# The last six rows of the first chunk's down projection as three float32r products each, and a new order of quarters in the second chunk

## The chip, the cores and the metric

The kernel runs on one core of one Trainium2 chip. The metric is the time of one execution on the device, in microseconds (us); the median of several runs is compared.

## What is computed

An mLSTM cell over 4 batches, 8 heads, 768 steps and a head width of 40, followed by a feed-forward block on its output: up projection (320 to 2048), exact GELU, down projection (2048 to 320).

```python
for t in range(S):                       # the cell, per batch and head
    m_new = np.maximum(f_gate[:, :, t] + m, i_gate[:, :, t])
    f_stab, i_stab = np.exp(f_gate[:, :, t] + m - m_new), np.exp(i_gate[:, :, t] - m_new)
    C = f_stab * C + i_stab * outer(v_t, k_t);  n = f_stab * n + i_stab * k_t
    y[:, :, t] = sigmoid(o_gate) * (C @ q_t) / np.maximum(np.abs(n @ q_t), 1.0)
x = y.transpose(0, 2, 1, 3).reshape(B * S, H * D)      # 3072 x 320
h = x @ w_in                                            # w_in 320 x 2048
g = 0.5 * h * (1.0 + erf(h / sqrt(2)))
out = g @ w_out                                         # w_out 2048 x 320
```

The weights come as 64-bit floats, which the kernel turns into 32-bit floats itself.

## The kernel before

The 768 steps are cut into 6 chunks of 128. For a chunk, the cell is computed in matrix form for each of the 4 batches: scores (q times k), a weight matrix W of exponentials that masks them, values (scores times v), a read of the state carried over from earlier chunks, and an update of that state. Its output y (128 steps x 4 batches = 512 columns) is turned by TensorE, which gives x, three row blocks (128, 128 and 64 rows, the last one twice) of 512 columns. Then come up, GELU and down of that chunk. The cell of a chunk runs between the matmuls of the feed-forward block of the chunk before it.

TensorE multiplies two kinds of data. Float32 operands are used in the cell and in part of the first chunk. The other matmuls use float32r, a rounded form; to keep the precision, a product is made as three float32r products: high part times high part, rest of x times high part of the weight, and x (rounded) times the low part of the weight. For that, x, g and the weights are split: ScalarE writes the high part (one cast), VectorE the rest (one subtract) and the rounded whole (one copy). Before, weights are scaled in the split and the outputs scaled back. Float32r matmuls read their moving operand in two interleaved halves and leave the result in that order; the output copies put it back.

w_in is held in 10 tiles (line 364), numbers 0 to 4 for the first half of the features and 5 to 9 for the second, where 2 and 7 hold the 64 remaining rows; two quarters of 512 features make a half. w_out is held as 16 rows, each the 128 x 320 block of 128 features, in four tiles of four rows (w_out0 to w_out3). Each weight piece is fetched by a DMA into one of four `bits` buffers (`fetch`, line 383) and turned to 32 bits by two ScalarE operations (`conv_one`, L402 and L403) and two VectorE operations (`conv_two`, L414 and L415), which also asks for a later piece.

The order of all work is written out by hand in strings, FRONT for the first stretch (the cell of chunks 0 and 1 and the feed-forward block of chunk 0), SECOND for the second chunk's block, LATER and LAST for the others. `play` (line 966) reads a string word by word and records the instructions of each word; every engine then runs its own instructions in that order and waits where data or a buffer is not ready. The letters that matter here:

- K and J: `conv_one` and `conv_two` of the next weight piece. Pieces 0 to 9 are w_in, 10 to 25 the rows of w_out.
- F: the next of the 16 rows of the first chunk's down (`first_down_steps`, line 850): four float32 matmuls of 128 x 320, one per batch, into four PSUM banks. After the last row ScalarE copies the banks out (L863) and the SP queue sends them.
- i: split of w_in tiles 5 to 9 into `hi_first` and in place (`split_first`, line 748); h: a copy of those high parts to their later place (`move_first`, L756); Z: split of w_in tiles 0 to 4 (`split_weight`, L745 and L746).
- a and b: high part and low part of a row of w_out (`out_hi`, L894, on ScalarE; `out_lo`, L901, on VectorE).
- u and f: parts of the first chunk's x, and quarters 2 and 3 of its up in float32r (the other two quarters are A and U, in float32).
- X and R: turning one batch of the second chunk's x (L695, with the high part by ScalarE, L705) and its rest and rounded whole (L716 and L717, on VectorE).
- B: the load of a 128 x 1024 tile of M for one batch, from which W is made (L208, L211); `<`: its mask on GpSimd (`mask`, L469); `>`: its 8 exponentials on ScalarE (`weights`, L495). In SECOND these are M and W.
- In SECOND: U, one quarter of up (`Chunk.up`, L920 and L926); g, the GELU of one of 16 rows (L933) and its parts (L934 to L936); d, one row of down with its 12 products (`product`, L940); S, scores of two batches (L567, L573); V, values of one batch (L657); C and h, read and update of the state (L620, L631); G, the sigmoid of the output gate (L505).

Exponentials, sigmoids and GELUs need different tables on ScalarE, so a table load stands at each change between them.

In PSUM, the up of a quarter holds four banks until its four GELUs have read them; in the second chunk, the scores of two batches and the values of batches 0 and 1 use the same banks next. The parts of g stand in a ring of 5 rows in the 16-place tile `g`, which in the first chunk holds the whole of g.

Of the kernel before, what the change touches and what calls it, by code (L numbers as in the profile page):

```python
# [19 lines left out]
BASE = 1.0 + 2.0 ** -12  # L20
LOW = 1.0 / 4097.0
# [10 lines left out]
    M3 f2 S2 V1 Y0 T3 J Y1 C2 e W3 K K K J S3 J C3 f3 K X0 B8 J K R0 B9 h5 J h6 h7 K J V2 K Y2 J J Z Z K  # L32
    K V3 X1 J K r F J h8 h9 (0 )0 F a0 a1 F K b0 b1 F a2 a3 F b2 b3 F F F J K X2 G3 F F J K J Y3 F J K R1 a4 a5 b4 b5 a6 b6 K B10 p + + + + F X3 a7 b7 F J J Z Z R2 R3
    a8 F [1 Z a9 a10 <0 <1 >0 >1 a11 a12 a13 a14 a15 b8 b9 b10 b11 b12 b13 b14 b15 B11 F F """
CELL = "MWGVYXRKQDCSht"
LATER = """
# [9 lines left out]
 U3 + M4 M5 Y0 Y1 D2 D3 K4 W4 W5 g12 t0 d8 g13 d9 g14 X0 t1 R0 d10 g15 X1 R1 C2 h2 O0 O1 d11 V2 Y2 t2 B6 J2 d12 V3 Y3 Q4 L5 B7 d13 X2 t3 R2 d14 X3 R3 d15 + O2 O3"""  # L46
# [8 lines left out]
def kernel(  # L55
# [398 lines left out]
    class Cell:  # L454
# [256 lines left out]
        def split_x(self, b):  # L711
            px = by_set(self.px.pop(b))
            if b == 0:
                parts["x_low"] = fars[0].tile([P, NX + 1, TG], F32R, name="x_low", tag="x_low", bufs=1)
            hi = in_place(parts["x"], b)
            nc.vector.tensor_tensor(out=in_place(parts["x_rest"], b), in0=px, in1=hi, op=OP.subtract)  # L716
            nc.vector.tensor_scalar(out=in_place(parts["x_low"], b), in0=px, scalar1=LOW, scalar2=None, op0=OP.mult)  # L717

# [5 lines left out]
    def products_begin():  # L724

        gate_ctx.close()
        pool = ctx.enter_context(tc.tile_pool(name="parts", bufs=1))
        hi_first.append(pool.tile([P, 5, 2, WP // 2], F32R, name="hi_first", tag="w_sums"))
        parts["x_rest"] = pool.tile([P, NX + 1, TG], F32R, name="x_rest")
        fars.extend([pool])  # L730
# [6 lines left out]
    def home(i):  # L737
        first = {1: 0, 4: 3, 6: 5, 9: 8, 7: 2}.get(i, i)
        if first not in hi_two:
            hi_two[first] = shared([P, 2, 2, WP // 2], F32R, "w_in_hi")  # L740
        return hi_two[first][:, int(i != first)]

    def split(i, w, to, lo):
        w_hi[i], w_lo[i] = to, lo
        nc.scalar.activation(out=to, in_=w, func=AF.Copy, scale=PART * 2.0 ** -12)  # L745
        nc.vector.scalar_tensor_tensor(out=lo, in0=to, scalar=-BASE * 2.0 ** 12, in1=w, op0=OP.mult, op1=OP.add)  # L746

# [6 lines left out]

    def move_first(i):
        nc.scalar.copy(out=home(i), in_=w_hi[i])  # L756
        w_hi[i] = home(i)
# [3 lines left out]
    def first_parts(k):  # L761
# [7 lines left out]
        nc.vector.tensor_scalar(out=parts["x_low"][:, k, :], in0=x, scalar1=LOW, scalar2=None, op0=OP.mult)  # L769

    def first_pair(k):
# [16 lines left out]
        for i in range(2):  # L788
            for e in range(2):
                nc.scalar.activation(out=first_g.t[:, HF * e + 2 * k + i, :].rearrange("p (a t) -> p a t", a=2),  # L790
                                     in_=pus[i][e].rearrange("p (t a) -> p a t", a=2), func=AF.Gelu, scale=4097.0)

    class Hidden:

        def __init__(self):
            self.t = gp.tile([P, NF, TG], F32, name="g", tag="g")

    def up_step(g, sets):
# [16 lines left out]
        for pu, (_, (i0, i1, t0, t1)) in zip(banks, sets):  # L815
            for e in range(2):
                nc.scalar.activation(out=g.t[:, i0 + HF * e:i1 + HF * e, t0:t1], in_=pu[e], func=AF.Gelu)
# [31 lines left out]

    def first_down_steps(g):  # L850
        po = []

        def row(n):

            f = feature[n]
            if n == 0:
                po.extend(ps_mm.tile([P, DM], F32, name="po", tag="ab"[b // 2]) for b in range(B))
            for b in range(B):
                nc.tensor.matmul(po[b], g.t[:, f, b * L:(b + 1) * L], w_row(n), start=(n == 0), stop=(n == NF - 1))  # L859
                if n == NF - 1:  # L860
                    if b % 2 == 0:
                        o_sb = outp.tile([P, 2, DM], F32, name="o_sb", tag="o_sb")
                    nc.scalar.copy(out=o_sb[:, b % 2, :], in_=po[b])  # L863
                    send(0, b, o_sb[:, b % 2, :])
# [3 lines left out]
    class Later:  # L868

        def __init__(self):  # L870
            self.w_hi, self.w_lo = {}, {}

        def begin(self):

            self.ring = gp.tile([P, NF, TG], F32R, name="g_parts", tag="g")

        def g_parts(self, n):

            i = 3 * (n % NM)
            return [self.ring[:, i + k, :] for k in range(3)]  # L880
# [4 lines left out]
        def out_hi(self, n):  # L885

            if n == 0:
                both = fars[0].tile([P, 8, DM], F32R, name="w_out_part", tag="w_sums")
                self.w_hi.update((i, both[:, 4 + i, :]) for i in range(4))
                self.w_lo.update((i, both[:, i, :]) for i in range(4))  # L890
            elif n not in self.w_hi:
                three = raw.tile([P, 3, DM], F32R, name="w_out_hi", tag="bits", bufs=NB)
                self.w_hi.update((n + i, three[:, i, :]) for i in range(3))
            nc.scalar.activation(out=self.w_hi[n], in_=w_row(n), func=AF.Copy, scale=PART * 2.0 ** -12)  # L894

        def out_lo(self, n):

            if n not in self.w_lo:
                four = const.tile([P, 4, DM], F32R, name="w_out_lo", tag=f"w_out{n // 4 - 1}")
                self.w_lo.update((n + i, four[:, i, :]) for i in range(4))  # L900
            nc.vector.scalar_tensor_tensor(out=self.w_lo[n], in0=self.w_hi[n], scalar=-BASE * 2.0 ** 12, in1=w_row(n), op0=OP.mult, op1=OP.add)  # L901

    class Chunk:

        def __init__(self, c, later):
            self.c, self.later, self.pus, self.po = c, later, {}, []
            self.side, self.main = [(((ps_mm, "b"), (ps_mm, "a")), ((ps_h, "h"), (ps_tr, "tr")))[(c + i) % 2] for i in (1, 0)]

        def up(self, q):

            at, r = [5 * (q // 2) + 3 * (q % 2) + x for x in range(NX)], 5 * (q // 2) + 2
# [10 lines left out]
            for i in range(2):  # L922
                for n in range(3):
                    for e in range(2):
                        h = halves[e]
                        nc.tensor.matmul(in_pairs(pus[i][e]), w3(r)[n][h, q % 2, i * P:(i + 1) * P], in_turns(x3[n][h, NX, :]),  # L926
                                         start=False, stop=(n == 2), skip_group_check=True)

        def gelu(self, n):
# [3 lines left out]
            nc.scalar.activation(out=whole, in_=self.pus[n // 4][n % 4 // 2][n % 2], func=AF.Gelu, scale=4097.0)  # L933
            nc.scalar.activation(out=hi, in_=whole, func=AF.Copy, scale=PART)  # L934
            nc.vector.tensor_tensor(out=rest, in0=whole, in1=hi, op=OP.subtract)  # L935
            nc.vector.tensor_scalar(out=low, in0=whole, scalar1=LOW, scalar2=None, op0=OP.mult)  # L936

        def product(self, n, t, k):
            x, w = self.later.g_parts(n)[k], self.later.w_parts(n)[k]
# [19 lines left out]
        def finish(self, t):  # L959
            if t % 2 == 0:  # L960
                self.o_sb = outp.tile([P, 2, DM], F32, name="o_sb", tag="o_sb")
            nc.scalar.activation(out=self.o_sb[:, t % 2, :].rearrange("p (a i) -> p a i", a=2),
                                 in_=self.po[t].rearrange("p (i a) -> p a i", a=2), func=AF.Copy, scale=4097.0)
# [21 lines left out]
    def first_blocks():  # L985
# [3 lines left out]
        for r in (32, 96):  # L989
# [12 lines left out]
                 u=first_parts, f=first_pair, i=split_first, h=move_first)  # L1002
# [52 lines left out]
```

## Time and profile before

| | |
|---|---|
| median of 3 runs | 441.36 us (440.73 to 442.05) |
| the profiled execution | 441.83 us |
| its span, first to last instruction | 440.0 us |
| granted TensorE clock, mean | 1.00 |

PE is TensorE's matmuls, PEld its weight loads, DVE VectorE, ACT ScalarE, POOL GpSimd, SPq the DMA queue that the sync engine issues. A row of a time line has the start in the span, the duration (of a run of equal instructions, from the first start to the last end), engine, line, operation, output and inputs, shapes, the count, and in brackets the idle time before it with what ended it. A row of the list of groups has the count, then total busy time, the mean of one in ns, and idle time before. PE's matmuls overlap, so their pace is read from start to start. A float32 matmul is recorded as two instructions, a float32r matmul as one.

### The profile page before, as it was taken

The page shows a single profiled execution, that of the slowest core. Times are in us where ns is not written, and L with a number is a line of the kernel's source. Part 1 is how long each engine was busy: PE and PEld are TensorE (multiplying, and loading weights), DVE is VectorE, ACT ScalarE, POOL GpSimd, SP SyncE. Part 2 cuts the span into 40 slices and gives each one's busy share as a digit, 9 for nine tenths or more (in the row PEclk, how much of TensorE's full clock was granted, in tenths as well). Part 3 has the DMA queues.
Part 4 walks back from the last instruction along what each step waited for, and adds up shares of the span by engine and source line. Part 5 has one row for each costly group of instructions (what it writes and reads, how often), then busy time and mean ns, then how long its engine had stood idle before and what let it go on. Part 6 is the DMA issues. An engine that isn't in the chain of part 4 may idle for free.

```text
span 440.0 us, 12965 instructions
## 1 busy us (share of the span) xinstructions
PE 431.5 (98%) x5320; PEld 374.9 (85%) x5320; DVE 289.4 (66%) x669; ACT 282.2 (64%) x603; POOL 48.7 (11%) x77
## 2 busy tenths in 40 slices
PE   8989999999999999999999999999999999999996
PEld 7778778877788898988898988898988898979986
DVE  8787777778958497837487837587746586533330
ACT  4979999957977977137977138976147915243441
POOL 3000221030020030120040130040010000000000
PEclk9999999999999999999999999999999999999999
DMA  7998996389951383474384564392552300010001
GB/s 156 205 198 229 214 240 150 85 267 226 201 130 50 69 192 66 106 164 84 62 170 74 104 164 76 62 186 34 106 145 29 48 16 1 17 46 0 1 2 60
DMA packets 162267, 48.81 MB, mean 111 GB/s; under 512 B 147776, under 2 KB 155232, under 8 KB 162208
## 3 DMA queue, kind: packets, MB, share of 16 engines
q1 hardware_dynamic: 161888, 47.65, 50.4%
q8 instruction: 42, 0.69, 0.7%
q10 hardware_dynamic: 320, 0.33, 0.2%
q14 instruction: 17, 0.14, 0.1%
HBM read 43.84 MB, written 9.37 MB: 121 GB/s over the span
## 4 chain that ended last, share of the span: by engine, by line
PE 88%; ACT 6%; DMA 2%; SPq 2%; issue 1%; DVE 1%; ACTq 0%; DVEq 0%
PE po L940 31%; PE pu L920 24%; PE po L859 8%; PE pu L926 7%; PE ph L657 3%; PE ps L567 3%; PE pu L780 2%; PE pf L620 2%; DMA bits<-in_moe_w_in_dram 2%; PE px L695 2%; ACT W L495 2%; SPq L173 1%; PE pf L631 1%; PE pt L529 1%; ACT pow L403 1%
## 5 line engine op out<-in xcount | busy, mean ns | idle before, releaser
L935 DVE TENSOR_TENSOR g_parts<-g_whole,g_parts 128x512 fp32r<-128x512 f32 x80 | 56.2, 702 | 68.9 <-ACT g_parts L934 66.3
L933 ACT ACTIVATE g_whole<-pu 128x512 f32<-128x512 f32 x80 | 47.1, 589 | 66.8 <-PE pu L926 54.4
L940 PE MATMUL po<-w_out_hi,g_parts 128*128 128x320 f32 x480 | 80.7, 308 | 0.0
L940 PEld LDWEIGHTS po<-w_out_hi,g_parts 128*128 128x128 f32 x480 | 67.9, 189 | 4.4 <-issue 3.3
L934 ACT ACTIVATE g_parts<-g_whole 128x512 fp32r<-128x512 f32 x80 | 50.5, 631 | 13.2 <-PE po L940 10.4
L920 PE MATMUL pu<-x_hi,w_in_hi 128*128 128x512 f32 x160 | 48.3, 384 | 0.0
L920 PE MATMUL pu<-x_rest,w_in_hi 128*128 128x512 f32 x160 | 47.6, 379 | 0.0
L940 PE MATMUL po<-w_out_lo,g_parts 128*128 128x320 f32 x240 | 44.4, 299 | 0.0
L469 POOL TENSOR_SCALAR_AFFINE_SELECT W<-W 128x1024 f32<-128x1024 f32 (+2 forms) x20 | 21.2, 1060 | 173.4 <-DMA W<-M_d 170.6
L495 ACT ACTIVATE W<-W,aT 128x128 f32<-128x128 f32 x128 | 38.9, 388 | 1.9 <-POOL W L469 1.8
L940 PEld LDWEIGHTS po<-w_out_lo,g_parts 128*128 128x128 f32 x240 | 36.4, 189 | 0.0
L940 PE MATMUL po<-w_out_part,g_parts 128*128 128x320 f32 x240 | 35.0, 303 | 0.0
L859 PE MATMUL po<-w_out,g 128*128 128x320 f32 x128 | 35.0, 432 | 0.0
L940 PEld LDWEIGHTS po<-w_out_part,g_parts 128*128 128x128 f32 x240 | 32.8, 189 | 1.9 <-issue 1.7
L936 DVE TENSOR_SCALAR g_parts<-g_whole 128x512 fp32r<-128x512 f32 x80 | 34.5, 431 | 0.0
L920 PEld LDWEIGHTS pu<-x_rest,w_in_hi 128*128 128x128 f32 x160 | 30.2, 189 | 4.3
L920 PEld LDWEIGHTS pu<-x_hi,w_in_hi 128*128 128x128 f32 x160 | 29.1, 189 | 3.9 <-issue 0.3
L859 PEld LDWEIGHTS po<-w_out,g 128*128 128x128 f32 x128 | 24.1, 190 | 9.7
L920 PE MATMUL pu<-x_low,w_in 128*128 128x512 f32 x80 | 23.8, 379 | 0.0
L920 PE MATMUL pu<-x_low,w_in_lo 128*128 128x512 f32 x80 | 23.8, 379 | 0.0
L402 ACT ACTIVATE sig<-bits 128x320 f32<-128x320 f32 (+1 forms) x26 | 15.2, 586 | 11.0 <-DMA bits<-in_moe_w_out_dram 5.2
L573 DVE TENSOR_TENSOR W<-ps,W 128x256 f32<-128x256 f32 (+1 forms) x48 | 17.7, 414 | 6.2 <-PE ps L567 6.0
(185 smaller groups left out, 737.0 us busy)
## 6 DMA issues: line engine op xcount, KB each, us to landing
W<-M_d SPq DMA_DIRECT2D x16, 512.0 KB, 5.8
bits<-in_moe_w_in_dram SPq DMA_DIRECT2D x20, 256.0 KB, 5.0
bits<-in_moe_w_out_dram SPq DMA_DIRECT2D x16, 320.0 KB, 5.1
blocks<-kq_d SPq DMA_DIRECT2D x32, 128.0 KB, 3.2
ob<-in_o_gate_dram SPq DMA_DIRECT2D x24, 160.0 KB, 4.4
out_dram<-o_sb SPq DMA_DIRECT2D x36, 80.0 KB, 2.0
wide<-M_d SPq DMA_DIRECT2D x4, 512.0 KB, 5.0
kq_d<-in_k_dram SPq DMA_DIRECT2D x6, 320.0 KB, 4.6
```

The costliest lines, as they stand in the source:

```text
L402: nc.scalar.activation(out=s, in_=hi.bitcast(F32), func=AF.Copy, scale=2.0 ** -112)
L469: nc.gpsimd.affine_select(out=x, in_=x, compare_op=OP.is_ge, fill=1.0e30, base=base, pattern=[[0, H], [1, x.shape[2]]], channel_multiplier=-1)
L495: nc.scalar.activation(out=W[n][:, h, :], in_=src, func=AF.Exp, scale=-1.0, bias=aT[:, self.c, r:r + 1])
L573: nc.vector.tensor_tensor(out=w[r, :, t], in0=ps[i][hip][r, :, t], in1=w[r, :, t], op=OP.mult)
L859: nc.tensor.matmul(po[b], g.t[:, f, b * L:(b + 1) * L], w_row(n), start=(n == 0), stop=(n == NF - 1))
L920: nc.tensor.matmul(in_pairs(pus[i][e]), w3(at[k])[n][:, e, i * P:(i + 1) * P], in_turns(x3[n][:, k, :]), start=(n == 0 and k == 0), stop=F ...
L926: nc.tensor.matmul(in_pairs(pus[i][e]), w3(r)[n][h, q % 2, i * P:(i + 1) * P], in_turns(x3[n][h, NX, :]), start=False, stop=(n == 2), skip ...
L933: nc.scalar.activation(out=whole, in_=self.pus[n // 4][n % 4 // 2][n % 2], func=AF.Gelu, scale=4097.0)
L934: nc.scalar.activation(out=hi, in_=whole, func=AF.Copy, scale=PART)
L935: nc.vector.tensor_tensor(out=rest, in0=whole, in1=hi, op=OP.subtract)
L936: nc.vector.tensor_scalar(out=low, in0=whole, scalar1=LOW, scalar2=None, op0=OP.mult)
L940: nc.tensor.matmul(in_pairs(self.po[t]), x[:, t * L:(t + 1) * L], in_turns(w), start=(n == 0 and k == 0), stop=(n == NF - 1 and k == 2), s ...
```

## The change

1. Rows 10 to 15 of the first chunk's down become three float32r products each. A new step z (`split_g`) makes the parts of one such row of g: one ScalarE cast and a VectorE subtract and copy, into tiles that take the places of quarters of g already used. The weights are the parts of w_out rows 10 to 15. Rows 0 to 9 stay float32, with w_out read in two interleaved halves, since all rows of a bank must leave the same order. The last row goes batch by batch.
2. g of the first chunk is four tiles of four rows instead of one of 16; so is the ring of parts later.
3. The second chunk takes the quarters of up in the order 2, 3, 0, 1, and the rows of w_out accordingly from 8 on. The first two use the w_in tiles 5 to 9, which are split before already; the five splits Z of tiles 0 to 4 move from FRONT into SECOND, three behind U1 and two behind g7. The high parts of tiles 5 to 9 keep a place of their own, and the five copies h are dropped.
4. The splits of w_out rows: 10 to 15 stand before the rows that use them, 8 and 9 at the end of FRONT, 0 to 7 in SECOND in instructions of one to three rows. FRONT has the conversions K and J closer together, with none of the splits between them.
5. The loads of M of batches 0 to 3 (B8 to B11) move behind the last weight fetch, and the exponentials of batches 0 and 1 from FRONT to SECOND, behind the first chunk's output copies. Turn X2 moves from behind row 7 to behind row 3, X3 from behind row 11 to behind row 8.
6. The scales in the splits and outputs (LOW, BASE, 4097) are dropped: the high part of a weight is a plain cast, its low part a plain subtract, the rounded whole a plain copy.

```diff
- ... K X0 B8 J K R0 B9 h5 J h6 h7 K J V2 K Y2 J J Z Z K
- K V3 X1 J K r F J h8 h9 (0 )0 F a0 a1 F K b0 b1 F a2 a3 F b2 b3 F F F J K X2 G3 F F J K J Y3 F J K R1 a4 a5 b4 b5 a6 b6 K B10 p + + + + F X3 a7 b7 F J J Z Z R2 R3
- a8 F [1 Z a9 a10 <0 <1 >0 >1 a11 a12 a13 a14 a15 b8 b9 b10 b11 b12 b13 b14 b15 B11 F F """
+ ... K X0 J K R0 J K J V2 K Y2 J J K
+ K V3 X1 J K r F J K (0 )0 F J K F J F X2 G3 F J K F Y3 R1 J K F p + + + + J F J a10,2 b10,2 z10 a12 b12 F X3 z11 F z12 a13,3 b13,3 F z13 F z14 R2 B8 B9 [1 F z15 R3 F <0 <1 a8 b8 B10 B11 F a9 b9 F"""
...
- U0 K1 Q1 L2 D0 D1 C0 h0 M2 M3 g0 g1 g2 g3 + +
- U1 g4 d0 g5 d1 g6 d2 g7 S0 d3 K2 Q2 L3 W2 W3 G0 G1 G2 G3 +
- U2 + g8 d4 g9 V0 V1 K3 Q3 B4 B5 J0 J1 d5 g10 d6 g11 S2 L4 d7
- U3 + M4 M5 Y0 Y1 D2 D3 K4 W4 W5 g12 t0 d8 g13 d9 g14 X0 t1 R0 d10 ...
+ U0 W0 W1 K1 Q1 L2 D0 D1 C0 h0 M2 M3 g0 g1 g2 g3 + +
+ U1 Z Z Z g4 d0 g5 d1 g6 d2 g7 Z Z S0 d3 K2 Q2 L3 W2 W3 G0 G1 G2 G3 +
+ U2 + g8 d4 g9 V0 V1 K3 Q3 B4 B5 J0 J1 d5 g10 d6 g11 a0,3 b0,3 S2 L4 d7
+ U3 + M4 M5 Y0 Y1 D2 D3 K4 W4 W5 a3 b3 g12 t0 d8 g13 a4,2 b4,2 d9 g14 X0 t1 R0 a6,2 b6,2 d10 ...
...
     def split(i, w, to, lo):
-        nc.scalar.activation(out=to, in_=w, func=AF.Copy, scale=PART * 2.0 ** -12)
-        nc.vector.scalar_tensor_tensor(out=lo, in0=to, scalar=-BASE * 2.0 ** 12, in1=w, op0=OP.mult, op1=OP.add)
+        nc.scalar.copy(out=to, in_=w)
+        nc.vector.tensor_tensor(out=lo, in0=w, in1=to, op=OP.subtract)
...
+    def split_g(n):
+        parts_of = []
+        for i in range(3 * len(first_parts_of), 3 * len(first_parts_of) + 3):
+            if i == len(singles):
+                four = gp.tile([P, 4, TG], F32R, name="g_part", tag=f"g{i // 4 % 3}")
+                singles.extend(four[:, j, :] for j in range(4))
+            parts_of.append(singles[i])
+        hi, rest, low = first_parts_of[n] = parts_of
+        whole = first_g.row(n)
+        nc.scalar.activation(out=hi, in_=whole, func=AF.Copy, scale=PART)
+        nc.vector.tensor_tensor(out=rest, in0=whole, in1=hi, op=OP.subtract)
+        nc.vector.tensor_copy(out=low, in_=whole)
...
-            for b in range(B):
-                nc.tensor.matmul(po[b], g.t[:, f, b * L:(b + 1) * L], w_row(n), start=(n == 0), stop=(n == NF - 1))
+            xs, ws = ((g.row(n),), (w_row(n),)) if n not in first_parts_of else (first_parts_of[n], later.w_parts(n))
+            steps = [(k, b) for k in range(len(xs)) for b in range(B)]
+            for k, b in sorted(steps, key=lambda x: x[::-1]) if n == NF - 1 else steps:
+                nc.tensor.matmul(in_pairs(po[b]), xs[k][:, b * L:(b + 1) * L], in_turns(ws[k]), start=(n == 0 and k == 0),
+                                 stop=(n == NF - 1 and k + 1 == len(xs)), skip_group_check=True)
...
+        def out_hi(self, n, k=1):
+            to = self.out_home(HI_AT[n], k)
+            self.w_hi.update((n + i, to[:, i, :]) for i in range(k))
+            nc.scalar.copy(out=to, in_=w_rows[n // 4][:, n % 4:n % 4 + k, :])
+
+        def out_lo(self, n, k=1):
+            to, hi = self.out_home(LO_AT[n], k), self.out_home(HI_AT[n], k)
+            self.w_lo.update((n + i, to[:, i, :]) for i in range(k))
+            nc.vector.tensor_tensor(out=to, in0=w_rows[n // 4][:, n % 4:n % 4 + k, :], in1=hi, op=OP.subtract)
...
+            self.first = 2 if c == 1 else 0
...
         def up(self, q):
-            at, r = [5 * (q // 2) + 3 * (q % 2) + x for x in range(NX)], 5 * (q // 2) + 2
+            p = (q + self.first) % 4
+            at, r = [5 * (p // 2) + 3 * (p % 2) + x for x in range(NX)], 5 * (p // 2) + 2
...
         def product(self, n, t, k):
-            x, w = self.later.g_parts(n)[k], self.later.w_parts(n)[k]
+            x, w = self.later.g_parts(n)[k], self.later.w_parts((n + 4 * self.first) % NF)[k]
```

More of the change, by code (lines that the diff above doesn't have):

```diff
@@ L768, in first_parts @@
         nc.vector.tensor_tensor(out=parts["x_rest"][:, k, :], in0=x, in1=hi, op=OP.subtract)
[L769 removed]
+        nc.vector.tensor_copy(out=parts["x_low"][:, k, :], in_=x)
     def first_pair(k):
@@ L882, in w_parts @@
         def w_parts(self, n):
             return self.w_hi[n], self.w_hi[n], self.w_lo[n]
[L885 to L894, printed above, removed]
```

71 lines of the change are left out of this document (41 added, 30 removed).

## The prediction, made before the changed kernel was run

> **What bounds the kernel now.** I read the page first (span, busy shares, chain), then a table by stage, then the time lines of TensorE, VectorE and ScalarE around the change.
>
> ```profile
> span 440.0 us, 12965 instructions
> ...
> PE 431.5 (98%) x5320; PEld 374.9 (85%) x5320; DVE 289.4 (66%) x669; ACT 282.2 (64%) x603; POOL 48.7 (11%) x77
> ...
> PE 88%; ACT 6%; DMA 2%; SPq 2%; issue 1%; DVE 1%; ACTq 0%; DVEq 0%
> ```
>
> ```profile
> 86.60:121.50 34.90, 34.90 (x137) 24.75 (x135) 28.98 (x64) 26.04 (x62) 4.53 (x5) 1.00 0.88 223
> 121.50:194.00 72.50, 72.50 (x962) 64.16 (x960) 48.92 (x111) 46.68 (x101) 10.62 (x14) 1.00 0.51 109
> ```
>
> The stage columns are the stretch, its length, then busy time of PE, PEld, DVE, ACT and POOL. 86.6 to 121.5 is the first chunk's down; the next row is the second chunk. PE is busy in all of both, at clock 1.00. So the time is TensorE's own work plus whatever makes it wait: what the change takes from PE is gained in full, and every wait it adds is lost in full.
>
> **The six rows on TensorE.** The down of the first chunk is 16 rows of w_out, each with 4 matmuls of 128x320; a float32 matmul leaves two records.
>
> ```profile
> 86.61 17.39 PE L859 MATMUL po<-w_out,g 128*128 128x320 f32 x64
> 103.84 0.38 PE L695 MATMUL px<-ident,ob 128*128 128x128 f32 x2
> ...
> 121.49 0.84 PE L920 MATMUL pu<-x_hi,w_in_hi 128*128 128x512 f32 x2
> ...
> 137.18 5.16 PE L940 MATMUL po<-w_out_part,g_parts 128*128 128x320 f32 x36
> 142.27 1.57 PE L567 MATMUL ps<-qT,kT 64*64 64x128 f32 x64
> ...
> 170.67 1.25 PE L940 MATMUL po<-w_out_hi,g_parts 128*128 128x320 f32 x8
> 171.75 0.71 PE L940 MATMUL po<-w_out_lo,g_parts 128*128 128x320 f32 x4
> 172.30 0.38 PE L695 MATMUL px<-ident,ob 128*128 128x128 f32 x2
> ```
>
> From start to start (a printed duration overlaps the next matmul), 64 records take 103.84 - 86.61 = 17.23 us: 32 matmuls at 0.538 us. The float32r product of the same shape is in the later chunks: 12 take 172.30 - 170.67 = 1.63 us, 0.136 each; 36 in a row take 5.09, 0.141 with an entry gap. Three products are 0.407 to 0.424 us. Removed: 24 matmuls, 12.92 us. Added: 72 products, 9.78 us (to 10.18). Gain 3.14 us, at least 2.74; I take 3.14, because these rows follow matmuls of the same 128 rows of the array.
>
> The Trainium skill (TensorE: Matmul & The Clock Gate, section Back-to-back issue gap) gives a sustained pace of about 81 ns at 128 columns and 131 ns at 512 in streams with weight loads. Halfway, an estimate of 106 ns for 320 columns, it would make the gain 24 x (0.538 - 0.318) = 5.3 us; the rows above measure 136 ns in just such a stream, so the trace disagrees.
>
> The ten rows that stay float32 now read w_out in two interleaved halves. No float32 matmul before does that. Bounds: nothing, since the products at L940 read so and run at 0.136; or half pace, 40 x 0.538 = 21.5 us. I take nothing: the float32 matmul takes four times as long over the same 320 columns, so it asks less of the read.
>
> **Whether the parts come in time.** Each of the six rows needs g split (one ScalarE cast, a VectorE subtract and copy), and w_out rows 10 to 15 split. In VectorE's order all of this stands behind the conversion of the last w_out row. That ends at 116.05 + 0.49 now:
>
> ```profile
> 91.44 1.37 DVE L677 SCALAR_TENSOR_TENSOR ob<-ob,den 128x320 f32<-128x320 f32 x1
> 93.17 0.49 DVE L414 SCALAR_TENSOR_TENSOR pow<-sig,pow 128x320 uint32<-128x320 uint32 x1 [0.37 <-ACT pow L403]
> ...
> 96.63 0.49 DVE L414 SCALAR_TENSOR_TENSOR pow<-sig,pow 128x320 uint32<-128x320 uint32 x1 [2.44 <-ACT pow L403]
> ...
> 97.99 1.28 DVE L746 SCALAR_TENSOR_TENSOR w_in_lo<-w_in_hi,w_in 128x512 fp32r<-128x512 f32 x2
> ...
> 103.36 0.90 DVE L901 SCALAR_TENSOR_TENSOR w_out_part<-w_out_part,w_out 128x320 fp32r<-128x320 f32 x2 [0.48 <-ACT w_out_part L894]
> 104.95 0.90 DVE L901 SCALAR_TENSOR_TENSOR w_out_part<-w_out_part,w_out 128x320 fp32r<-128x320 f32 x2 [0.69 <-ACT w_out_part L894]
> ...
> 112.39 1.29 DVE L901 SCALAR_TENSOR_TENSOR w_out_lo<-w_out_hi,w_out 128x320 fp32r<-128x320 f32 x3
> 114.19 0.49 DVE L901 SCALAR_TENSOR_TENSOR w_out_lo<-w_out_hi,w_out 128x320 fp32r<-128x320 f32 x1 [0.52 <-ACT w_out_hi L894]
> ...
> 116.05 0.49 DVE L415 SCALAR_TENSOR_TENSOR w_out<-sig,pow 128x320 uint32<-128x320 uint32 x1
> ...
> 118.60 0.55 DVE L716 TENSOR_TENSOR x_rest<-px,x_hi 128x384 fp32r<-128x384 f32 x1
> 119.06 0.55 DVE L717 TENSOR_SCALAR x_low<-px 128x384 fp32r<-128x384 f32 x1
> ```
>
> ```profile
> 92.16 0.50 ACT L402 ACTIVATE sig<-bits 128x320 f32<-128x320 f32 x1 [2.73 <-DMA bits<-in_moe_w_out_dram]
> ```
>
> ```profile
> 85.12 1.80 SPq L211 DMA_DIRECT2D W<-M_d  x1
> ```
>
> ```profile
> L935 DVE TENSOR_TENSOR g_parts<-g_whole,g_parts 128x512 fp32r<-128x512 f32 x80 | 56.2, 702 | 68.9 <-ACT g_parts L934 66.3
> ...
> L936 DVE TENSOR_SCALAR g_parts<-g_whole 128x512 fp32r<-128x512 f32 x80 | 34.5, 431 | 0.0
> ```
>
> The change takes from VectorE ahead of that point: two w_in splits (1.28) and eight w_out splits (0.90 + 0.90 + 1.29 + 0.49 = 3.58) with their ScalarE waits (0.48 + 0.69 + 0.52 = 1.69): 6.55 us. The two waits of 0.37 and 2.44 are for w_out data, late behind the two 512 KB loads of W that the SP queue issues first; these loads move behind the last w_out fetch, another 2.81. So the last conversion should end at 116.5 - 9.4 = 107.1. Behind it stand, from start to start: three split instructions for six rows (0.90 + 0.49 + 1.29 = 2.7 at most), five subtract-and-copy pairs before the last one and that one (6 x 0.95 = 5.7, by 702 and 431 ns less the overlap of neighbours), and one x split (0.95): 9.35 us, so the last row's parts are there at 116.5. PE comes to that row at 121.5 - 3.1 - 1.63 = 116.7 and needs the third part some 0.3 later. It fits, with 0.5 us to spare; earlier rows have as much or more, and the last x split is done at 117.4, when the second chunk's up starts at 118.4. Cost taken: nothing. If the conversion ends later than 107.6, each us costs one. Dropping the five moves of w_in parts and moving the W exps only frees ScalarE. The tiles of g that the parts are written to come free in time: the last one needs PE's row 12, whose second product ends near 113.0, and VectorE asks for it at 115.5.
>
> One thing may eat this slack: a W mask on GpSimd, next to which a 0.49 us operation took 1.37 (the first row above, beside the row below). The mask starts 6.25 us after its load is issued (85.12 to 91.37); the loads move behind the last x load, to about 108, and so the masks to about 114, beside the last parts: 0 to 1 us, in the rival on lateness.
>
> ```profile
> 91.37 1.09 POOL L469 TENSOR_SCALAR_AFFINE_SELECT W<-W 128x1024 f32<-128x1024 f32 x1 [23.95 <-DMA W<-M_d]
> ```
>
> **What the second chunk pays.** Quarters 2 and 3 first means that the five w_in splits of quarters 0 and 1 are done inside it: three casts ahead of gelu 4 on ScalarE, two behind gelu 7.
>
> ```profile
> 87.76 1.67 ACT L756 CAST w_in_hi<-hi_first 128x512 fp32r<-128x512 f32 x3
> ...
> 101.71 1.12 ACT L756 CAST w_in_hi<-hi_first 128x512 fp32r<-128x512 f32 x2
> ...
> 133.98 0.60 ACT L933 ACTIVATE g_whole<-pu 128x512 f32<-128x512 f32 x1 [3.62 <-DVE g_parts L936]
> ...
> 136.64 0.60 ACT L933 ACTIVATE g_whole<-pu 128x512 f32<-128x512 f32 x1 [0.24 <-PE pu L926]
> ...
> 141.35 0.63 ACT L934 ACTIVATE g_parts<-g_whole 128x512 fp32r<-128x512 f32 x1 [0.51 <-PE po L940]
> 142.00 1.28 ACT L495 ACT_TABLE_LOAD   x1
> ...
> 152.24 0.60 ACT L933 ACTIVATE g_whole<-pu 128x512 f32<-128x512 f32 x1
> 152.87 0.63 ACT L934 ACTIVATE g_parts<-g_whole 128x512 fp32r<-128x512 f32 x1
> 153.41 0.58 ACT L933 ACTIVATE g_whole<-pu 128x512 f32<-128x512 f32 x1
> ```
>
> ```profile
> 154.09 1.33 PEld L657 LDWEIGHTS ph<-vb,W 128*32 128x32 f32 x128 [0.17 <-ACT g_whole L933]
> ```
>
> The casts cost 1.67 + 1.12 = 2.79 us. ScalarE has 0.24 + 0.51 us of waits in that stretch, and small ones of some 0.2 in all, so the table load at 142.00 slips by 1.8. The scores step, which starts at 142.27, takes the bank of gelu 7: that ended at 141.35 - 0.51 = 140.84, and 1.67 - 0.24 - 0.2 = 1.2 later is 142.1, just in time. From there to gelu 8 at 152.24 ScalarE runs without a wait (exps, sigmoids, two more table loads). The values step at L657, 64 matmuls for each of two batches, takes the PSUM banks of gelu 8 and 9: gelu 8 ends at 152.84, 1.25 before the first batch starts; gelu 9 at 153.99, and the second batch starts half of 1.33 us into the step, at 154.76, 0.77 later. A slip of 1.8 passes both: 0.55 us on the first, 1.0 on the second in all. I add 1.0 for a PE wait there, with 0 (casts hidden) and 1.8 (whole slip) as its ends. What is late next, the gelus 10 and 11, waits for PE already, so it moves with PE; nothing more is lost.
>
> The W exps of batches 0 and 1 (16, with two table loads) now run behind the first chunk's output copies, which makes gelus 0 and 1 some 1.8 later; the 3.62 us that ScalarE waits at 133.98 cover it. The splits of w_out rows 0 to 9 that move into the last two quarters stand before gelus whose data PE brings later still. Scales that fall away, and copies in place of scaled copies of the same shape, I put at nothing.
>
> **Sum.** -3.14 + 1.0 = -2.1 us. The profiled execution's span goes from 440.0 to 437.9; it took 441.83 in all, 0.47 over the median of 441.36. Against the median: 439.3 us.
>
> **Rivals.**
> 1. The casts are hidden, PE doesn't wait at the values step: 441.36 - 3.14 = 438.2. For it: ScalarE's other small gaps in 136 to 142. Against: the 0.77 us of slack is short against 2.79 us of casts. 0.14.
> 2. The parts come 0.5 to 3 us late (masks on GpSimd, data of the last w_out rows, which now wait on 8 rotating DMA slots): 439.8 to 442.3, middle 441.0. For it: only 0.5 us to spare. Against: two of the added splits are wide instructions and cheaper than the sum has them. 0.20.
> 3. Slower: the last w_out conversion does not move forward, since the fetches and not VectorE pace it, and stays near 116.5. Then everything behind it ends at 125.9, the second chunk's up starts at 127.2 instead of 121.5, and with 1.0 the time is 441.36 + 5.7 + 1.0 = 448.1. It decides from 109.7 (no gain left); 0.3% slower from 111.0. For it: ScalarE's waits for data of 2.73 us (92.16). Against: they sit right behind the W loads, which go. 0.12.
> 4. The products don't pay: paced by their weight loads they would take 3 x 0.189 = 0.567 us, more than 0.538.
>
> ```profile
> L940 PEld LDWEIGHTS po<-w_out_hi,g_parts 128*128 128x128 f32 x480 | 67.9, 189 | 4.4 <-issue 3.3
> ```
>
> Then 24 x 0.029 = 0.7 is lost: 441.36 + 0.7 + 1.0 = 443.1. Against it: twelve loads in 1.63 us, so loads overlap. With the interleaved float32 reads (up to 441.36 - 2.1 + 21.5 = 460.8): 0.04.
>
> **How the numbers follow.** The sum 0.50 (its own range 438.7 to 439.9), rivals 0.14, 0.20, 0.12 and 0.04. The predicted time is the sum's. The range 438.0 to 441.6 takes in the sum, rival 1 and most of rival 2, about 0.8. 0.3% is 1.3 us, about what a measurement tells from no change: faster means under 440.0. Faster: 0.50 less 0.02, 0.14, and 0.05 of rival 2: 0.67. Same: 0.02 and most of rival 2 with a little of rival 3: 0.18. Slower: 0.15.
>
> **What would show it.** Right: 72 products in about 9.8 us behind ten rows at 0.538 x 4; the second chunk's first up 3.1 us earlier, at 118.4; ScalarE's table load before the second pair of W exps slipping by 1.8 against PE; a PE wait of about 1 us in all at the values step, put down to g_whole; then a constant distance to the end. Wrong: PE waits for g_part or w_out_part in the first chunk's down (rival 2 or 3, by where the last w_out conversion ends: 107 or 116), no wait at the values step (rival 1), or float32 rows slower than 2.15 us each (rival 4).

## The result, and the profile after

| | before | after |
|---|---|---|
| median, compared on one chip | 441.0 us (5 runs) | 446.89 us (5 runs) |
| ratio after to before | | 1.0124, interval 1.0105 to 1.0143 |
| the profiled execution, its span | 441.83, 440.0 us | 446.04, 444.3 us |

The change makes the kernel 1.24% slower (4.6 to 6.3 us); the forecast was 439.3 us. The page of after, its span and its busy times:

```profile
span 444.3 us, 13025 instructions
...
PE 435.9 (98%) x5344; PEld 376.6 (85%) x5344; DVE 296.6 (67%) x674; ACT 283.1 (64%) x597; POOL 50.3 (11%) x77
```

PE is busy 4.4 us longer than before (431.5), though the six rows should have taken 3.1 us from it. Where that is, TensorE's time line of the first chunk's down shows, matmuls first and then weight loads (start, duration, engine, line, operation, shapes, count, idle time before):

```profile
86.04 11.04 PE L878 MATMUL po<-w_out,g 128*128 128x320 f32 x32
96.91 0.38 PE L697 MATMUL px<-ident,ob 128*128 128x128 f32 x2
...
97.24 13.76 PE L878 MATMUL po<-w_out,g 128*128 128x320 f32 x40
110.83 0.38 PE L697 MATMUL px<-ident,ob 128*128 128x128 f32 x2
```

```profile
85.93 0.64 PEld L878 LDWEIGHTS po<-w_out,g 128*128 128x128 f32 x3
...
113.53 0.19 PEld L878 LDWEIGHTS po<-w_out_part,g_part 128*128 128x128 f32 x1
113.87 8.34 PEld L878 LDWEIGHTS po<-w_out_part,g_part 128*128 128x128 f32 x61
122.46 1.38 PEld L878 LDWEIGHTS po<-w_out_part,g_part 128*128 128x128 f32 x10 [0.24 <-DVE g_part L866]
123.79 0.33 PEld L952 LDWEIGHTS pu<-x_hi,hi_first 128*128 128x128 f32 x2
```

32 records of the float32 rows take 96.91 - 86.04 = 10.87 us, 40 take 13.59: 0.340 a record, 0.680 a matmul, where it was 0.538. Ten rows are 40 matmuls, so 40 x 0.142 = 5.7 us are lost. The 72 products take 123.79 - 113.53 = 10.26 us with one wait of 0.24, so 0.139 each: the gain of the six rows is there, 12.92 - 10.02 = 2.9 us. The down as a whole, from its first weight load to that of the second chunk's first up, grows from 34.95 to 37.86 us (before: the first two of the three rows below; after: 85.93 to 123.79).

```profile
86.51 3.53 PEld L859 LDWEIGHTS po<-w_out,g 128*128 128x128 f32 x14
...
121.46 0.46 PEld L920 LDWEIGHTS pu<-x_hi,w_in_hi 128*128 128x128 f32 x2
...
162.03 0.33 PEld L920 LDWEIGHTS pu<-x_hi,w_in_hi 128*128 128x128 f32 x2
```

A second loss lies in the second chunk: from its first up (U0) to its fourth (U3) it took 162.03 - 121.46 = 40.57 us and takes 42.55. After's weight loads, with the waits, then VectorE and GpSimd there:

```profile
147.97 0.30 PEld L952 LDWEIGHTS pu<-x_hi,w_in_hi 128*128 128x128 f32 x2 [0.36 <-PE po L972]
...
156.78 0.69 PEld L659 LDWEIGHTS ph<-vb,W 128*32 128x32 f32 x64 [0.28 <-ACT g_whole L965]
157.93 0.69 PEld L659 LDWEIGHTS ph<-vb,W 128*32 128x32 f32 x64 [0.46 <-ACT g_whole L965]
...
166.34 0.30 PEld L952 LDWEIGHTS pu<-x_hi,w_in_hi 128*128 128x128 f32 x2 [1.05 <-PE po L972]
```

```profile
145.81 1.29 DVE L748 TENSOR_TENSOR w_in_lo<-w_in,w_in_hi 128x512 fp32r<-128x512 f32 x2
147.11 3.08 DVE L575 TENSOR_TENSOR W<-ps,W 128x256 f32<-128x256 f32 x8
...
162.58 1.57 DVE L967 TENSOR_TENSOR g_parts<-g_whole,g_parts 128x512 fp32r<-128x512 f32 x1
...
164.42 1.14 DVE L931 TENSOR_TENSOR w_out_part<-w_out,w_out_part 128x960 fp32r<-128x960 f32 x1
165.49 1.40 DVE L575 TENSOR_TENSOR W<-ps,W 128x256 f32<-128x256 f32 x4
```

```profile
162.48 1.14 POOL L471 TENSOR_SCALAR_AFFINE_SELECT W<-W 128x1024 f32<-128x1024 f32 x1 [27.26 <-DVE g_parts L967]
```

The wait at the values (156.78 and 157.93) was forecast. Those at U2 (147.97) and U3 (166.34) were not: quarters U2 and U3 use the PSUM banks of the scores, which come free when VectorE has multiplied them into W (L575; PE's own row of U3 names that line), and now a w_in split (1.29 us) and a w_out split (1.14 us) stand ahead of these multiplies. At 162.58 a subtract, 0.69 us elsewhere, also takes 1.57 beside a GpSimd mask.

A third thing went wrong without costing much yet. ScalarE and VectorE in the conversion of the last w_out rows, and the SP queue:

```profile
98.35 0.49 ACT L404 ACTIVATE sig<-bits 128x320 f32<-128x320 f32 x1 [2.45 <-DMA bits<-in_moe_w_out_dram]
...
101.52 0.49 ACT L404 ACTIVATE sig<-bits 128x320 f32<-128x320 f32 x1 [2.21 <-DMA bits<-in_moe_w_out_dram]
...
107.91 0.50 ACT L404 ACTIVATE sig<-bits 128x320 f32<-128x320 f32 x1 [2.99 <-DVE w_out L417]
```

```profile
109.45 0.49 DVE L417 SCALAR_TENSOR_TENSOR w_out<-sig,pow 128x320 uint32<-128x320 uint32 x1
```

```profile
90.13 1.74 SPq L173 DMA_DIRECT2D wide<-in_k_dram  x2
91.92 1.31 SPq L173 DMA_DIRECT2D vb<-in_v_dram  x2
93.34 1.07 SPq L175 DMA_DIRECT2D ob<-in_o_gate_dram  x1
94.50 0.56 SPq L394 DMA_DIRECT2D bits<-in_moe_w_out_dram  x1
...
98.73 4.13 SPq L175 DMA_DIRECT2D ob<-in_o_gate_dram  x1
102.96 0.57 SPq L394 DMA_DIRECT2D bits<-in_moe_w_out_dram  x1
```

The last conversion ends at 109.94, not at 107.1: ScalarE still waits 2.45 and 2.21 us for w_out. In front of the fetch at 94.50 and those behind it stand loads of k, v and the gate for a later chunk (from 90.13). Another gate load, at 98.73, stands in front of the last fetch, but both waits were over before that fetch was issued at 102.96, and the last conversion, at 107.91, waited for VectorE; that this load cost anything is not shown. PE came to row 10 only at 113.5, so the delay stayed hidden behind the slow float32 rows.

Two stages, then: +2.91 in the down and +1.98 in the second chunk, 4.9 us; the stretch before the down was 0.58 shorter in this execution (85.93 against 86.51), which gives the span's 4.3; from U3 to the end both take 278.0 us.

### The profile page after: what moved, and what is told of

The parts are those of the page before. It is cut to its first block, busy times and chain, and to the rows that moved or that the text cites. A ratio compares the mean times of both kernels' runs of the same rounds, so it can differ in the third digit from the quotient of the medians.

```text
span 444.3 us, 13025 instructions
## 1 busy us (share of the span) xinstructions
PE 435.9 (98%) x5344; PEld 376.6 (85%) x5344; DVE 296.6 (67%) x674; ACT 283.1 (64%) x597; POOL 50.3 (11%) x77
## 4 chain that ended last, share of the span: by engine, by line
PE 85%; ACT 8%; DVE 3%; issue 2%; DMA 1%; SPq 1%; DVEq 0%; ACTq 0%
PE po L972 29%; PE pu L952 22%; PE po L878 8%; PE pu L958 6%; PE ph L659 3%; PE pu L778 2%; PE ps L569 2%; ACT W L497 2%; PE pf L622 2%; PE px L697 2%; PE pu L809 2%; PE pf L633 1%; PE cold L250 1%; DMA ob<-in_o_gate_dram 1%; PE ps L553 1%
## 5 line engine op out<-in xcount | busy, mean ns | idle before, releaser
L972 PE MATMUL po<-w_out_part,g_parts 128*128 128x320 f32 x960 | 143.8, 304 | 0.0
L972 PEld LDWEIGHTS po<-w_out_part,g_parts 128*128 128x128 f32 x960 | 131.8, 189 | 6.4 <-issue 4.6
L968 DVE CAST g_parts<-g_whole 128x512 fp32r<-128x512 f32 x80 | 34.7, 434 | 0.0
L952 PE MATMUL pu<-x_hi,w_in_hi 128*128 128x512 f32 x80 | 24.4, 386 | 1.0 <-DVE W L575 0.8
L878 PEld LDWEIGHTS po<-w_out,g 128*128 128x128 f32 x80 | 15.0, 190 | 11.1
L952 PE MATMUL pu<-x_hi,hi_first 128*128 128x512 f32 x80 | 23.9, 380 | 0.0
L952 PE MATMUL pu<-x_rest,hi_first 128*128 128x512 f32 x80 | 23.8, 379 | 0.0
L952 PE MATMUL pu<-x_rest,w_in_hi 128*128 128x512 f32 x80 | 23.8, 379 | 0.0
L575 DVE TENSOR_TENSOR W<-ps,W 128x256 f32<-128x256 f32 (+1 forms) x48 | 17.7, 413 | 4.5 <-PE ps L569 4.3
L707 ACT ACTIVATE x_hi<-px 128x384 fp32r<-128x384 f32 x20 | 9.8, 491 | 16.3 <-PE px L697 15.8
L416 DVE SCALAR_TENSOR_TENSOR pow<-sig,pow 128x320 uint32<-128x320 uint32 (+1 forms) x26 | 15.5, 595 | 5.1 <-ACT pow L405 5.1
```

Source lines behind the costliest of these rows:

```text
L416: nc.vector.scalar_tensor_tensor(out=p, in0=s, scalar=3, in1=p, op0=OP.logical_shift_left, op1=OP.bitwise_or)
L575: nc.vector.tensor_tensor(out=w[r, :, t], in0=ps[i][hip][r, :, t], in1=w[r, :, t], op=OP.mult)
L878: nc.tensor.matmul(in_pairs(po[b]), xs[k][:, b * L:(b + 1) * L], in_turns(ws[k]), start=(n == 0 and k == 0), stop=(n == NF - 1 and k + 1 = ...
L952: nc.tensor.matmul(in_pairs(pus[i][e]), w3(at[k])[n][:, e, i * P:(i + 1) * P], in_turns(x3[n][:, k, :]), start=(n == 0 and k == 0), stop=F ...
L968: nc.vector.tensor_copy(out=low, in_=whole)
L972: nc.tensor.matmul(in_pairs(self.po[t]), x[:, t * L:(t + 1) * L], in_turns(w), start=(n == 0 and k == 0), stop=(n == NF - 1 and k == 2), s ...
```

## The experiments

The table holds, for each, the ratio of its time to that of before on the same chip with its interval, the down (first weight load of row 0 to that of U0) and the stretch from U0 to U3, both from the profiled execution. The times differ from what the two stages add up to by up to 1.1 us: even in before and versions 1 and 2, whose program is the same up to there, the down begins between 86.5 and 88.9 us. So costs of 1 us and less are read from the stages.

| version | ratio | down, us | U0 to U3, us |
|---|---|---|---|
| before | 1 | 34.95 | 40.57 |
| after | 1.0124 (1.0105 to 1.0143) | 37.86 | 42.55 |
| 1 before, rows read interleaved | 1.0212 (1.0175 to 1.0250) | 43.92 | 40.64 |
| 2 before, rows read evens, then odds | 1.0039 (1.0021 to 1.0058) | 36.34 | 40.71 |
| 3 after, float32 rows read in order | 1.0055 (1.0029 to 1.0080) | 34.52 | 42.55 |
| 4 after, whole down in order | 1.0048 (1.0028 to 1.0068) | 35.21 | 42.55 |
| 5 after, splits behind the scores | 1.0065 (1.0043 to 1.0088) | 37.59 | 41.43 |
| 6 as 3 and 5, later loads | 0.9941 (0.9923 to 0.9960) | 31.95 | 42.37 |
| 7 as 3 and 5, w_in splits early | 0.9990 (0.9968 to 1.0012) | 34.87 | 40.55 |
| 8 all repairs (3, 5, 6, 7) | 0.9922 (0.9900 to 0.9945) | 31.95 | 40.44 |
| 9 as 8, whole down in order | 0.9939 (0.9912 to 0.9966) | 32.73 | 40.49 |
| 10 as 8, float32 rows interleaved | 1.0077 (1.0049 to 1.0105) | 37.59 | 40.47 |
| 11 before, later loads | 0.9998 (0.9984 to 1.0013) | 34.96 | 40.68 |

**1. Is it the read?** The kernel before, with nothing but the read (and the columns put back in the output copy):

```diff
- nc.tensor.matmul(po[b], g.t[...], w_row(n), start=(n == 0), stop=(n == NF - 1))
+ nc.tensor.matmul(in_pairs(po[b]), g.t[...], in_turns(w_row(n)), start=(n == 0), stop=(n == NF - 1), ...)
```

> The kernel before with one thing of the change alone: all 16 float32 rows of the first chunk's down read w_out in two interleaved halves (and the output copies put the columns back). Theory (the interleaved read is what slows the float32 matmul, from 0.538 to 0.68 us): 64 matmuls take 0.142 us more each, the stretch from the first of them to the second chunk's first up grows by 9.1 us, and the time goes from 441.0 to about 450. Rival (the read costs nothing, and the slow rows in the changed kernel come from what runs beside them there, DMA or VectorE): the rows stay at 0.538 us and the time stays within 0.5 us of 441.0.

```profile
89.02 21.91 PE L859 MATMUL po<-w_out,g 128*128 128x320 f32 x64
110.77 0.38 PE L695 MATMUL px<-ident,ob 128*128 128x128 f32 x2
```

The interleaved read takes columns 0, 160, 1, 161 and so on. 64 records take 21.75 us: 0.680 a matmul, as in after, with everything around it as in before. The down grows by 8.97 us, the time by 9.4 (451.71 against 442.31). The rival, that something beside them slows the rows, falls.

**2. What in the read?** The same with another order of the columns, 0, 2, 4 and so on, then 1, 3, 5:

```diff
+ nc.tensor.matmul(po[b].rearrange("p (a t) -> p a t", a=2), ..., w_row(n).rearrange("p (t a) -> p a t", a=2), ...)
```

> The kernel before, its 16 float32 rows reading w_out as all even columns and then all odd ones (steps of 8 bytes, never alternating between two places 640 bytes apart). Theory A (any step other than to the next word slows the float32 read): a matmul takes about 0.68 us as with the interleaved halves, and the time is about 9 us above that of before. Theory B (only the alternation between two distant places costs): 0.538 us and no change. A value between would say that the two effects add.

```profile
87.59 18.09 PE L859 MATMUL po<-w_out,g 128*128 128x320 f32 x64
105.52 0.38 PE L695 MATMUL px<-ident,ob 128*128 128x128 f32 x2
```

17.93 us for 32 matmuls, 0.560 each. Steps of 8 bytes cost 0.022 us, alternating between places 640 bytes apart 0.142: neither theory holds alone, but most of the loss comes with the alternation. Other distances than 640 bytes were not tried, so whether the distance matters is open.

The Trainium skill (Advanced Engine Details and Errata, section Memory Cachelines) says that SBUF is read in lines of 16 bytes and that a read keeps its pace if the next access falls into the same line. By that rule the halves hit a new line at every element and the evens every second time, and the float32 times of these two runs agree with it (0.142 and 0.022 lost). The float32r products of runs 8 and 9 below do not: 0.138 in halves, 0.149 in order.

**3. Can the rows be mended alone?** In after, the ten float32 rows read in order and write PSUM in the interleaved order:

```diff
+ if len(xs) == 1:
+     nc.tensor.matmul(po[b].rearrange("p (t a) -> p a t", a=2), xs[k][...], ws[k].rearrange("p (a t) -> p a t", a=2), ...)
+     continue
```

> The changed kernel, its ten float32 rows reading w_out in order again and writing PSUM in the interleaved order instead, so that the 72 products can add to them unchanged. Theory: the cost sits on the side of the read, the 40 matmuls go back to 0.538 us and 5.7 us are given back; since PE then comes to the six rows at about 107.8 and not 113.5, it waits 0 to 2.5 us for their parts (the last w_out conversion ended at 109.9): 441.2 to 443.7. Rival (any order of the columns that is not the same on both sides slows the float32 matmul): no gain, 446.9.

```profile
86.94 8.78 PE L879 MATMUL po<-w_out,g 128*128 128x320 f32 x32
95.56 0.38 PE L697 MATMUL px<-ident,ob 128*128 128x128 f32 x2
...
107.44 0.41 PE L697 MATMUL px<-ident,ob 128*128 128x128 f32 x2 [0.62 <-DVE x_low L719]
...
110.47 0.81 PE L882 MATMUL po<-w_out_part,g_part 128*128 128x320 f32 x4 [0.36 <-ACT g_part L864]
111.72 8.15 PE L882 MATMUL po<-w_out_part,g_part 128*128 128x320 f32 x58 [0.44 <-DVE g_part L865]
120.03 1.63 PE L882 MATMUL po<-w_out_part,g_part 128*128 128x320 f32 x10 [0.17 <-DVE g_part L866]
```

8.62 us for 16 matmuls, 0.539 each: for this matmul the read side is what costs; writing PSUM in steps costs nothing. Of the 5.7 us the down gives back only 3.3 (37.86 to 34.52): PE now comes to row 10 at about 109.9 and waits for the parts. The late conversions are laid bare. The time is 2.2 us over before (444.50 against 442.31 here).

**4. And the float32r products?** In after, all of the first down in order (`po[b]`, `ws[k]` as they are).

> The changed kernel with the whole first down, the float32 rows and the 72 float32r products, reading w_out in order and writing PSUM in order. Theory (only the float32 rows are slow when interleaved, the products take 0.136 us either way): the same as the run with the float32 rows alone put in order, 441.2 to 443.7. Rival (the products need the interleaved read for their pace): they take longer than 0.136 us each, and every 0.01 us more costs 0.72 us.

The same time as run 3, but 68 products took 9.94 us, 0.146 each, against 0.139: the rival has a part of it. Run 9 repeats this where no wait is mixed in.

**5. What delays U2 and U3?** In after, the last two w_in splits and the VectorE half of the first w_out split moved behind the scores (S0, S2) in SECOND:

```diff
- ... d2 g7 Z Z S0 d3 ...      ... g11 a0,3 b0,3 S2 L4 d7
+ ... d2 g7 S0 Z Z d3 ...      ... g11 a0,3 S2 L4 b0,3 d7
```

> The changed kernel with two steps of the second chunk behind the scores step and not ahead of it: the last two w_in splits, and the VectorE half of the first w_out split. Theory (the waits of 0.4 us at quarter U2 and 1.1 us at U3 come from VectorE, which does these splits ahead of the multiplies of the scores that free the PSUM banks): both waits go, up to 1.3 us are gained, 445.6 to 446.0. Rival (the banks are late for another reason, ScalarE's gelus or the GpSimd masks): the waits stay and so does the time, 446.9.

```profile
157.62 0.81 PE L659 MATMUL ph<-vb,W 128*32 128x41 f32 x64 [0.42 <-ACT g_whole L965]
158.76 0.81 PE L659 MATMUL ph<-vb,W 128*32 128x41 f32 x64 [0.34 <-ACT g_whole L965]
```

Both waits at U2 and U3 are gone, U0 to U3 falls by 1.12 us to 41.43. (The time is 3.1 us over before, 445.40 against 442.31, where after has 5.9; the two stages account for 1.4 of that gain.) What stays, 0.86 over before, is the wait at the values (above).

At U3 the split does not act alone. The multiplies start 3.36 us after the scores in after, with a wait of 1.05 on the weight loads; 3.18 after them in run 6 below, with 0.88; 1.66 in run 5, with none. From these, an estimate: the first 2.3 us are free. The w_out split is 1.07 of after's 3.36 us and the stretch of the subtract 0.88, so either alone would have cost 0.2 at most. In run 5 the split is moved, and the mask falls later too (164.15, beside no subtract).

**6. Why are the parts late?** Runs 3 and 5 together, and the loads that turns X1 and X2 issue put behind the fetch of the last w_out row:

```diff
- if self.c == 1 and b < NQ: load(n + NLD, 1, 3)
- if self.c == 1: load(n + NLD, 3, 4)
+ if self.c == 1:
+     put_off.extend([lambda: load(n + NLD, 1, 3)] * (b < NQ) + [lambda: load(n + NLD, 3, 4)])
+     if b in (0, NQ): run_off()
...
- ... X2 G3 F J K F Y3 R1 J ...
+ ... X2 G3 F J ] K F Y3 R1 J ...          # ]: run_off
```

> The changed kernel with the float32 rows reading in order (as in the run before), the second chunk's two steps moved behind the scores step (as there), and the loads of the chunk after next that the output turns X1 and X2 issue moved on the SP queue behind the fetch of the last w_out row. Theory (the parts of rows 10 to 15 come late because those loads hold up the w_out fetches, so that ScalarE and VectorE wait some 3 us for data): the last w_out conversion ends at 107 to 108 and not at 110.2, PE's waits of some 2.7 us in front of and within the products fall to under 0.5, and against the kernel before the time is 1 to 2 us shorter, about 440.5 where before takes 442. Rival (VectorE's own queue sets the end of the conversions, not the data): the conversions end at 109.5 or later, the waits stay, and the time is 0.5 to 1.5 us longer than that of before.

```profile
105.54 0.49 DVE L417 SCALAR_TENSOR_TENSOR w_out<-sig,pow 128x320 uint32<-128x320 uint32 x1
```

```profile
107.69 10.18 PE L888 MATMUL po<-w_out_part,g_part 128*128 128x320 f32 x72
...
159.97 0.67 PE L962 MATMUL pu<-x_hi,w_in_hi 128*128 128x512 f32 x2 [0.66 <-DVE W L581]
```

The last conversion ends at 106.03, the 72 products run without a wait, and the down falls to 31.95, 3.00 under before. The time is 2.3 us under before (439.28 against 441.57), a little more than expected. A wait of 0.66 is back at U3, though no split stands there. By the trace, the masks on GpSimd now fall beside VectorE's two copies ahead of the multiplies, which take 1.31 us each instead of 0.42 (no run moves the masks alone; in run 8 the mask starts at 157.21, behind both copies, and the wait is gone):

```profile
156.03 1.31 DVE L978 CAST g_parts<-g_whole 128x512 fp32r<-128x512 f32 x1
...
157.87 1.31 DVE L978 CAST g_parts<-g_whole 128x512 fp32r<-128x512 f32 x1
```

```profile
155.47 1.59 POOL L477 TENSOR_SCALAR_AFFINE_SELECT W<-W 128x1024 f32<-128x1024 f32 x1 [26.48 <-PE po L982]
157.79 1.90 POOL L477 TENSOR_SCALAR_AFFINE_SELECT W<-W 64x1024 f32<-64x1024 f32 x2 [0.72 <-DMA W<-M_d]
```

**7. What does the values step wait for?** Runs 3 and 5 together, with the five w_in splits at the end of FRONT, where ScalarE waits for PE, and none in SECOND:

```diff
- ... B10 B11 F a9 b9 F
+ ... B10 B11 F a9 b9 Z Z Z Z Z F
...
- U1 Z Z Z g4 d0 g5 d1 g6 d2 g7 S0 Z Z d3 ...
+ U1 g4 d0 g5 d1 g6 d2 g7 S0 d3 ...
```

> The changed kernel with the float32 rows reading in order, the VectorE half of the first w_out split behind the scores step, and all five w_in splits of quarters 0 and 1 done at the end of the first chunk's down, where ScalarE waits 4 to 5 us for PE, and not within the second chunk. Theory (the five casts, 2.8 us of ScalarE, make gelus 8 and 9 late and cost PE 0.7 to 1 us at the values step): the two PE waits put down to g_whole go, the stretch from the second chunk's first up to its U3 goes back from 41.4 to 40.6 us as in the kernel before, and the time is within 0.5 us of before's (442). Rival (the casts only fill gaps; the gelus are late because of PE or VectorE): the stretch stays at 41.4 and the time is 1 us above before's.

```profile
153.69 1.56 PE L659 MATMUL ph<-vb,W 128*32 128x41 f32 x128
```

One run of 128 matmuls without a wait, and U0 to U3 is 40.55, as before. So the five splits cost 0.88 us there (run 5 against 7). Their subtracts on VectorE move as well; that it is the casts is read from the two waits, put down to ScalarE's g_whole.

**8. All repairs together.**

> All three: float32 rows reading in order, the five w_in splits at the end of the first chunk's down with the first w_out split behind the scores step, and the later loads behind the last w_out fetch. If the three costs (interleaved reading 5.7 us, late parts 2.7, waits in the second chunk 2.0) are separate and complete, what is left is the gain of the six rows, 24 x 0.538 - 72 x 0.136 = 3.1 us: 2 to 3.1 us under before, about 439.5 where before takes 442. If one of them only moves the wait elsewhere, the time stays within 1 us of before's.

```profile
108.85 9.97 PEld L888 LDWEIGHTS po<-w_out_part,g_part 128*128 128x128 f32 x72
118.76 0.33 PEld L962 LDWEIGHTS pu<-x_hi,hi_first 128*128 128x128 f32 x2
```

438.63 us against 441.57, 0.78% faster than before, the lowest ratio here, though its interval overlaps those of versions 6 and 9. The down is 3.00 us shorter, the second chunk as long as before to 0.13 us: the three costs were all there was in these two stages.

**9 and 10. Each read order, with nothing else in the way.** Version 8 with the whole down in order:

> The version with all three repairs, but the whole first down reading and writing in order, its 72 float32r products too. Theory (a float32r product loses without the interleaved read what the float32 matmul wins: in the run with everything in order 68 products took 9.94 us, 0.146 each, against 0.139 interleaved): no wait hides it now, the 72 products take about 10.5 us and not 9.95, and the time is 0.5 us above that of the version with all three. Rival (the 0.146 came from waits within that run): the products take 9.95 us and the time is the same.

```profile
108.47 10.73 PEld L884 LDWEIGHTS po<-w_out_part,g_part 128*128 128x128 f32 x72
119.17 0.33 PEld L957 LDWEIGHTS pu<-x_hi,hi_first 128*128 128x128 f32 x2
```

72 products in 10.70 us against 9.91 in version 8: 0.149 against 0.138. The down is 0.78 longer; in the time the difference lies within the intervals. Version 8 with the float32 rows interleaved as in the change:

> The version with all three repairs, but its ten float32 rows reading in two interleaved halves again, as in the change. Theory (the cost of the read adds to whatever else holds): the first down grows from 31.95 to 37.6 us, 40 x 0.142 = 5.7 more, and the time is about 2.8 us above that of before, 0.6% slower. Rival (with the waits gone, part of it is hidden): less than 1 us above before.

```profile
88.27 0.64 PEld L884 LDWEIGHTS po<-w_out,g 128*128 128x128 f32 x3
...
125.86 0.32 PEld L958 LDWEIGHTS pu<-x_hi,hi_first 128*128 128x128 f32 x2
```

The down is 37.59, 5.64 more than in version 8, and the time 2.7 us over before (444.86 against 442.19). The interleaved read alone makes the change a loss.

**11. Do the later loads pay by themselves?** The kernel before, with the loads of run 6 put off in the same way.

> The kernel before with the loads of the output turns X1 and X2 moved on the SP queue behind the fetch of the last w_out row, and nothing else. Theory (the order of the loads matters only because the six rows need their parts by 107 us; in the kernel before PE never waits there): no change, within 0.3% of before. Rival (the later loads are a gain by themselves, and the best version owes its time to them and not to the six rows): 1 us or more under before.

No change (442.17 against 442.47). The later loads are no gain here by themselves.

## Why the prediction was wrong

- **The float32 rows: wrong, and the step that failed.** "I take nothing: the float32 matmul takes four times as long over the same 320 columns, so it asks less of the read." It was 5.7 us (run 10: 5.64; run 1: 0.680 against 0.538 a matmul). The products at L940, which read that way at full pace, were taken as a witness for another data type. The term had a bound of 21.5 us and hung on no row of its kind, yet it was given a chance of 0.04.
- **The gain of the six rows: right.** 3.14 was forecast (2.74 at least), 2.9 measured in after and 3.00 in the down of version 8.
- **The parts in time: wrong by its reason, hidden in after.** The forecast let the waits for w_out go with the W loads; the loads of k, v and the gate stand on the SP queue as well, and the waits stayed (2.45 and 2.21). The end was 109.94, near the "no gain left" of rival 3. It is worth 34.52 - 31.95 = 2.6 us where the rows run at full pace (run 3 against 6); in after PE was late enough not to see more than 0.24. The mask that the forecast feared did come, at 116.78: from there to 122.4 two subtracts and two copies of g, beside masks and multiplies on GpSimd, took 4.80 us instead of 2.22, and the 0.24 follows them. No run shows anything of the "8 rotating DMA slots" of rival 2.
- **The wait at the values: right.** 1.0 forecast, 0.88 by runs 5 and 7, at the place and for the tile (g_whole) that were named.
- **The splits costed at nothing: wrong.** Each was weighed against the gelus behind it on ScalarE; the scores' multiplies, behind it on VectorE, were not looked at. 1.12 us (run 5), at U3 together with the mask.
- **Sum.** -2.9 + 5.7 + 0.2 in the down (measured +2.91, by rounded terms) and 0.88 + 1.12 in the second chunk, where -3.14 + 1.0 was forecast. With the read alone mended the change still does not win (run 3, 1.0055), because the late parts then come out and the second chunk's 1.98 stays.

## What to carry to other kernels

Cost an operand's read order for the data type that will use it: here the order that gains a float32r product 0.01 us costs a float32 matmul 0.14. When work moves, look at what stands behind it on every engine that it uses and at whose bank or buffer that frees, and when a stage is to begin earlier, follow its data back to the queue that fetches it and list everything issued ahead. A cost hidden behind another one comes out when that one is mended, so repairs are best tried together as well as alone.

## What the runs showed of the hardware

- A float32 matmul of 128 x 320 takes 0.538 us with the moving operand in order, 0.560 at steps of 8 bytes, 0.680 alternating between halves 640 bytes apart. A float32r product of that shape goes the other way: 0.149 in order, 0.138 alternating. Why float32r gains from it was not tried.
- The order of the writes to PSUM did not matter to the float32 matmul: 0.539 us with every second word written (run 3). The Trainium skill (Advanced Engine Details and Errata, section Memory Cachelines) says that any non-contiguous pattern in PSUM slows matmuls significantly; this run does not agree.
- Beside a GpSimd mask a VectorE subtract took 1.57 us instead of 0.69 and a copy 1.31 instead of 0.42: 0.88 and 0.89 more, the same for the longer and the shorter operation. Such a copy stands ahead of the multiplies in before too (159.29) and costs nothing there; two of them in run 6 go with a wait of 0.66.
